# Reordering the opening of a pre-norm attention and GEGLU kernel: who makes the statistics, the masks and the first v tiles

## The chip, the cores and the metric

The kernel runs on one core of a Trainium2 chip. A core has five engines with a queue of instructions each: TensorE (PE in the profile, with PEld for its weight loads), VectorE (DVE), ScalarE (ACT), GpSimd (POOL) and SyncE (SP), which here only issues DMAs. Each engine works through its queue in order and waits on semaphores that others raise. The metric is the device time of one execution in microseconds. Before the change it is 279.58 us, the median of 3 runs (279.43 to 279.63).

## The reference

One layer over x of 2048 tokens by D = 640, in bf16, with 32 heads of Dh = 20 and a hidden width of 1536:

```python
qkv = layernorm(x) @ wqkv                     # split in q, k, v, per head
pq, pk = q_head @ w_phi[h], k_head @ w_phi[h] # a 20 x 20 matrix for each head
phi = concat(softmax(p), softmax(-p))         # for q and for k
kv  = sum over tokens of phi_k^T v            # per head, and z = sum of phi_k
o   = (phi_q kv) / (phi_q z + 1e-6)
h   = x + o @ wo
out = h + (gelu(ln(h) @ w_gate) * (ln(h) @ w_up)) @ w_down
```

## The kernel before

The tokens are cut into 16 tiles of 128. A tile is normalised with tokens on the partitions, transposed into `LN1T` (one buffer for four tiles), and then multiplied with weights. The 20 x 20 matrices of all heads are folded into the weights first: a block-diagonal matrix `BD` is made from w_phi and a mask (`bd`, L385), and `fold` (L214) multiplies the transposed weight (`WkT`, `WqT`) with it, 128 rows of the weight at a time (d = 0 to 4), six matmuls each. The result in PSUM (`wa`) is cast into `Wk2` or `Wq2` by ScalarE where d is in `KA` or `QA`, else by VectorE.

The order of work is written out by hand. Each engine gets its instructions in the order of the Python program, so the order of the calls sets what stands behind what on every queue. The part that the change touches is the opening (L394 to L430) and the loop over tiles (L435 to L482):

- Statistics. Tiles 0 and 1 (`ln_0`), and 2, 4, 5, 6, 7 (`ln_st`) get mean and variance from VectorE (`bn_stats`, L110, and the aggregate, L114). The reciprocal root is made by ScalarE for tiles 0 to 2 (L119, L120) and by GpSimd for the others (L122, L123). Tile 3 is different: `st3_act` (L369) lets ScalarE sum the squares and then the values of the tile (L372, the sums come out as `sm3`), and GpSimd makes mean and reciprocal root of them in five small steps (L374 to L378).
- Normalising and transposing. `ln_ap` (L257) lets VectorE (L139) or ScalarE (L134) write the normalised tile. `ln_tp` (L264) transposes it on TensorE (five matmuls against the identity, L147) into PSUM, from where ScalarE or, with a second argument of True, VectorE copies it into `LN1T` (L148). From tile 6 on the transposing is a DMA of the SP queue instead (L150).
- v. `v_part` (L284) issues the v matmuls of a tile for some of the five 128-row slices of the weight, `v_mm` (L279) all ten; `v_ev` (L293) lets ScalarE move the result to `vS`.
- Loads. SP issues the loads of x, W_v and w_phi in order (L171 to L181), then five DMA transposes of W_k (`load_T`, L186), then the rest of x (L417 to L419).
- PSUM. The tiles `tp`, `pv`, `pk`, `wa` take turns in four buffers (three from pass 4 on). A matmul into a buffer waits until the buffer's last contents have been read.
- The loop. Pass t runs k of tile t (`k_tile`, L302; ScalarE makes both exponentials, L307), a fold of W_q in the passes listed in `FQ`, accumulations of kv for earlier tiles in the passes of `KVG` (L340), v of tile t + 4, the normalising of tile t + 6 on ScalarE and its transpose on SP, the statistics of tiles t + 8 and t + 9 in even passes, and `k_norm` (L310), in which VectorE sums and inverts and VectorE and GpSimd multiply (L322). In passes 0 to 4 it also loads and transposes a slice of W_q (L464).

After the loop come the q products, attention and the feed-forward part (L615, L636), which the change does not touch.

Of the kernel before, what the change touches and what calls it, by code (L numbers as in the profile page):

```python
# [10 lines left out]
ALU = mybir.AluOpType  # L11
# [6 lines left out]
def kernel(  # L18
# [12 lines left out]
    nc = tc.nc  # L31
    P = 128
# [15 lines left out]
    VP = (0, 2, 4, 6, 9, 11)  # L48
    KA, QA = (1,3), (0,1,2,3,4)
    FQ = (4, 5, 6, 7, 8)  # L50

# [124 lines left out]
    nc.sync.dma_start(x_sb[0][:, 2:3, :], x_v[:, 2:3, :])  # L176
    nc.sync.dma_start(Wv[:, 2:4, :], w_v[:, 2:4, 2 * D:3 * D])
    nc.sync.dma_start(wphi, phi_v.rearrange("(c p) f -> p c f", p=P))
    nc.sync.dma_start(Wv[:, 4:5, :], w_v[:, 4:5, 2 * D:3 * D])
    nc.sync.dma_start(x_sb[0][:, 3:4, :], x_v[:, 3:4, :])  # L180
    nc.sync.dma_start(x_sb[1][:, 0:2, :], x_v[:, 4:6, :])  # L181
# [102 lines left out]
    def v_part(t, *cs):  # L284

        if 0 in cs:
            pv[t] = gtile("pv")
        for c in cs:
            for u in range(2):
                nc.tensor.matmul(pv[t][:, u, 0:HD], lhsT=lnT(t, c), rhs=Wv[:, c, u * HD:(u + 1) * HD],  # L290
                                 start=(c == 0), stop=(c == NC - 1))
# [77 lines left out]
    def st3_act(i):  # L369

        xt = x_sb[0][:, 3, :]
        nc.scalar.activation(sq3, xt, (ACTF.Square, ACTF.Identity)[i], accum_out=sm3[:, i:i + 1])  # L372
        if i == 1:
            nc.gpsimd.tensor_scalar(v3[:, 0:1], sm3[:, 1:2], sm3[:, 1:2], -1.0 / (D * D), op0=ALU.mult, op1=ALU.mult)  # L374
            nc.gpsimd.tensor_scalar_add(v3[:, 0:1], v3[:, 0:1], EPS)
            nc.gpsimd.tensor_scalar(v3[:, 1:2], sm3[:, 0:1], 1.0 / D, v3[:, 0:1], op0=ALU.mult, op1=ALU.add)
            nc.gpsimd.tensor_tensor(v3[:, 2:3], v3[:, 1:2], nhalf[:, 0:1], op=ALU.pow)
            nc.gpsimd.tensor_scalar(v3[:, 3:4], sm3[:, 1:2], 1.0 / D, None, op0=ALU.mult)  # L378
            lnp[3] = xt, v3[:, 3:4], v3[:, 2:3], None
# [4 lines left out]

    def bd(c0, c1):  # L385

        n = c1 - c0
        nc.vector.tensor_tensor(BD[:, c0:c1], wphi[:, c0:c1, None, :].to_broadcast([P, n, 8, Dh]),
                                hmask[:, c0:c1, :, None].to_broadcast([P, n, 8, Dh]), ALU.mult)

    def tr_c(t):
        transpose_to(LN1T[0][:, :, t * P:(t + 1) * P], xc[t], True, t == 1)
# [6 lines left out]
    v_part(0, 0, 1)  # L399
    tr_c(1)  # L400
    st3_act(0)
    v_part(0, 2, 3)
    bd(0, 3)
    ln_ap(2, on_pe=True)
    bd(3, NC)
    st3_act(1)
    v_part(1, 0, 1, 2, 3)
    ln_tp(2, True)
    v_part(0, 4)
    v_ev(0)  # L410
    ln_st(4, act=False)
    ln_ap(3, on_pe=True)
    v_part(1, 4)
    v_ev(1)
    v_part(2, *range(NC))
    v_ev(2)
    nc.sync.dma_start(x_sb[1][:, 2:4, :], x_v[:, 6:8, :])  # L417
    nc.sync.dma_start(x_sb[2], x_v[:, 8:12, :])
    nc.sync.dma_start(x_sb[3], x_v[:, 12:16, :])  # L419
    fold(WkT, Wk2, False, (0, 1, 2))  # L420
    ln_tp(3, False)
    fold(WkT, Wk2, False, (3, 4))
    v_mm(3)
    v_ev(3)
    ln_ap(4, on_pe=True)
    ln_tp(4)
    ln_st(5, act=False)
    ln_st(6)
    ln_ap(5, on_pe=True)
    ln_st(7)  # L430
# [4 lines left out]
    for t in range(NT):  # L435
# [14 lines left out]
        for i in KVG.get(t, ()):  # L450
            kv_tile(i)
        if t + 4 < NT:
            v_mm(t + 4)
            if t == 0:
                ln_tp(5)
        if t > 0 and t + 6 < NT:
            ln_ap(t + 6, on_act=True)
        if t + 4 < NT:
            v_ev(t + 4)
        if t % 2 == 0 and t + 8 < NT:  # L460
            ln_st(t + 8, t + 9)
        k_norm(t)
        if t < NC:
            load_T(WqT, 0, t)  # L464
        if t == 10:
# [299 lines left out]
```

## Time and profile before

| | |
|---|---|
| median of the runs | 279.58 us |
| span of the profiled execution, first to last instruction | 277.2 us |
| the median less the span | 2.4 us |
| PE, DVE, ACT, POOL busy, share of the span | 98%, 60%, 52%, 34% |
| granted TensorE clock in all slices | full |

For the profiled execution the profile gives the span as its own time; what lies around the span (launch and end) is known only as the difference to the median. A busy PE is not PE at its peak: a matmul's recorded duration holds the pipeline's latency, and two that follow each other overlap. So the starts of the groups are to be compared, not their durations. In a line of the timeline stand the start and the duration in us, the engine, the source line, the operation, output and input tiles with shapes, the count, and in brackets the idle time before it and what ended that. DMAs are told by the time from issue to landing.

### The profile page before, as it was taken

What the parts mean: (1) busy time and instruction counts of PE and PEld (TensorE: products, weight loads), DVE (VectorE), ACT (ScalarE), POOL (GpSimd) and SP (SyncE); (2) the same over time, 40 slices, a digit from 0 to 9 for tenths busy, and PEclk for the clock granted to TensorE, in tenths of its full rate; (3) what the DMA queues carried; (4) which work ended last, traced back from release to release, by engine and by line L of the source; (5) the groups of instructions that cost most, each with busy time, mean ns of one, the idle gap of its engine ahead of it and who ended that gap; (6) DMA issues with size and microseconds to landing.
All of it is one profiled execution on the core that took longest, in us unless ns stands there. A gap on an engine that the chain in (4) does not pass through costs nothing.

```text
span 277.2 us, 5817 instructions
## 1 busy us (share of the span) xinstructions
PE 271.6 (98%) x2337; PEld 172.1 (62%) x2337; DVE 167.3 (60%) x292; ACT 143.5 (52%) x239; POOL 94.7 (34%) x213
## 2 busy tenths in 40 slices
PE   7899999999999999999999999999999999999995
PEld 3677777764555887788754555675455567444574
DVE  6799999899496776675325757322666622233222
ACT  4879998778598755374524364413445440222200
POOL 4348997765202217365301353400226230000000
PEclk9999999999999999999999999999999999999999
DMA  7965732489730021324120213130022413000011
GB/s 204 192 232 112 99 74 47 44 256 393 255 102 0 4 47 36 85 49 77 30 65 2 47 27 63 32 88 33 14 36 25 73 25 95 26 0 0 0 50 47
DMA packets 42235, 21.37 MB, mean 77 GB/s; under 512 B 35040, under 2 KB 40416, under 8 KB 42208
## 3 DMA queue, kind: packets, MB, share of 16 engines
q1 hardware_dynamic: 42208, 21.01, 30.8%
q8 instruction: 18, 0.29, 0.5%
q14 instruction: 9, 0.07, 0.1%
HBM read 10.18 MB, written 2.62 MB: 46 GB/s over the span
## 4 chain that ended last, share of the span: by engine, by line
PE 87%; SPq 3%; DMA 3%; DVE 2%; ACT 2%; issue 1%
PE gu L615 38%; PE pd L636 19%; PE pq L362 8%; PE po L570 8%; PE pk L274 5%; PE pv L274 4%; PE ab L510 3%; PE kvp L340 2%; SPq L186 2%; DMA LN1T<-ln 2%; DVE stats L110 1%; DMA WkT<-in_A_wqkv_dram 1%; ACT E L307 1%; ACT ln L134 1%; PE wa L228 1%
## 5 line engine op out<-in xcount | busy, mean ns | idle before, releaser
L621 DVE TENSOR_TENSOR GT<-gu,g 128x512 bf16<-128x512 f32 (+1 forms) x60 | 34.4, 580 | 54.3 <-ACT g L618 54.1
L618 ACT ACTIVATE g<-gu 128x512 bf16<-128x512 f32 (+1 forms) x60 | 30.7, 512 | 69.3 <-PE gu L615 68.5
L615 PE MATMUL gu<-LN2T,Wg 128*128 128x512 bf16 (+1 forms) x300 | 61.9, 337 | 0.1
L615 PE MATMUL gu<-LN2T,Wu 128*128 128x512 bf16 (+1 forms) x300 | 61.8, 337 | 0.0
L636 PE MATMUL pd<-Wd,GT 128*128 128x320 bf16 (+2 forms) x396 | 53.8, 295 | 0.0
L636 PEld LDWEIGHTS <-GT 128*128 128x128 bf16 x396 | 37.9, 98 | 15.3 <-DVE GT L621 0.9
L615 PEld LDWEIGHTS <-Wu 128*128 128x128 bf16 x300 | 29.3, 98 | 22.6
L615 PEld LDWEIGHTS <-Wg 128*128 128x128 bf16 x300 | 28.3, 98 | 20.8
L274 PEld LDWEIGHTS <-LN1T 128*128 128x128 bf16 x290 | 27.9, 98 | 11.0 <-DMA LN1T<-ln 0.3
L322 POOL TENSOR_TENSOR vt<-vS,rs 128x672 bf16<-128x672 bf16 x22 | 29.1, 1344 | 9.1 <-DVE rs L318 7.4
L641 DVE TENSOR_TENSOR y<-pd,x_sb 128x640 bf16<-128x640 f32 (+3 forms) x18 | 13.5, 749 | 30.2 <-PE pd L636 30.2
L518 ACT COPY AB<-ab 128x704 f32<-128x704 f32 x28 | 19.6, 748 | 19.8 <-PE ab L510 19.6
L551 DVE TENSOR_TENSOR tt<-AB,w 128x1280 bf16<-128x1280 f32 x16 | 23.8, 1486 | 1.0 <-POOL w L544 0.9
L570 PE MATMUL po<-Wo,oT 128*128 128x320 bf16 x160 | 24.3, 299 | 0.0
L274 PE MATMUL pk<-Wk,LN1T 128*128 128x320 bf16 x160 | 24.0, 299 | 0.0
L314 DVE TENSOR_REDUCE sk<-E 128x64 f32<-128x1280 bf16 x16 | 22.9, 1434 | 1.2 <-ACT E L307 1.2
L362 PE MATMUL pq<-LN1T,Wq 128*128 128x512 bf16 x100 | 22.9, 379 | 0.0
L367 ACT ACTIVATE Eq<-pq 128x1024 bf16<-128x1024 f32 (+1 forms) x26 | 19.9, 830 | 2.4 <-PE pq L362 2.4
L307 ACT ACTIVATE E<-pk 128x640 bf16<-128x640 f32 x28 | 18.3, 716 | 4.5 <-PE pk L274 4.3
L570 PEld LDWEIGHTS <-oT 128*128 128x128 bf16 x160 | 15.6, 98 | 7.0 <-ACT oT L148 0.3
L274 PE MATMUL pv<-Wv,LN1T 128*128 128x320 bf16 x130 | 19.8, 299 | 0.2 <-DMA LN1T<-ln 0.2
L134 ACT ACTIVATE ln<-x_sb,v,rstd 128x640 bf16<-128x640 bf16 x14 | 12.9, 919 | 11.3 <-POOL v L598 11.1
(101 smaller groups left out, 268.1 us busy)
## 6 DMA issues: line engine op xcount, KB each, us to landing
out_dram<-y SPq DMA_DIRECT2D x15, 160.0 KB, 1.8
Wg<-in_B_w_gate_dram SPq DMA_DIRECT2D x1, 1920.0 KB, 9.4
Wu<-in_B_w_up_dram SPq DMA_DIRECT2D x1, 1920.0 KB, 15.3
Wd<-in_B_w_down_dram SPq DMA_DIRECT2D x1, 1920.0 KB, 7.9
x_sb<-in_A_x_dram SPq DMA_DIRECT2D x2, 640.0 KB, 5.5
Wo<-in_A_wo_dram SPq DMA_DIRECT2D x1, 800.0 KB, 11.1
x_sb<-in_A_x_dram SPq DMA_DIRECT2D x4, 160.0 KB, 3.1
Wv<-in_A_wqkv_dram SPq DMA_DIRECT2D x2, 320.0 KB, 4.1
```

The lines of the kernel that those rows point to most:

```text
L274: nc.tensor.matmul(ps[:, u, 0:HD], lhsT=lnT(t, c), rhs=W[:, c, u * HD:(u + 1) * HD], start=(c == 0), stop=(c == NC - 1))
L307: nc.scalar.activation(Ek[t][:, s, :].rearrange("p (u f) -> p u f", u=2), pk[:, :, 0:HD], ACTF.Exp, scale=((lnp[t][2], nrstd[t]) if t in C ...
L314: nc.vector.reduce_sum(sk, Ek[t].rearrange("p s (h f) -> p (s h) f", f=Dh), axis=AX.X)
L322: eng.tensor_tensor(vt[:, s], vS[t % 8], rs[:, s * H:(s + 1) * H, None].to_broadcast([P, H, VC]), ALU.mult)
L362: nc.tensor.matmul(pqs[j][:, i, :], lhsT=Wq2[:, kc, c * P:(c + 1) * P], rhs=LN1T[b][:, kc, :], start=(kc == 0), stop=(kc == NC - 1))
L367: nc.scalar.activation(Eq[j][:, :, s, :], pqs[j][:, 0:len(QG[j])], ACTF.Exp, scale=(1.0, -1.0)[s])
L551: nc.vector.tensor_tensor(tt.rearrange("p s (h f) -> p s h f", f=Dh), num, w[:, :, :, None].to_broadcast([P, 2, H, Dh]), ALU.mult)
L570: nc.tensor.matmul(po[:, u, 0:HD], lhsT=st[t][:, c, :], rhs=Wo[:, c, u * HD:(u + 1) * HD], start=(c == 0), stop=(c == NC - 1))
L615: nc.tensor.matmul(gu[:, i, 0:n], lhsT=W[:, c, f * P:(f + 1) * P], rhs=LN2T[b][:, c, a0:a1], start=(c == 0), stop=(c == NC - 1))
L618: nc.scalar.activation(g[:, 0:n], gu[:, 0, 0:n], ACTF.Gelu_apprx_tanh)
L621: nc.vector.tensor_tensor(st[b, "g", f][:, a0:a1], gu[:, 1, 0:n], g[:, 0:n], ALU.mult)
L636: nc.tensor.matmul(pd[:, u, n0:n1], lhsT=st[b, "g", f][:, tl * P:(tl + 1) * P], rhs=Wd[:, f, u * HD + n0:u * HD + n1], start=(f == 0), sto ...
```

## The change

- `st3_act`: ScalarE makes the sum of tile 3 first and the squares second. GpSimd's steps that need the sum alone (its square, the constant, the mean) are issued after the first; those that need the squares (the variance, the power) after the second.
- On SP, x of tile 3 is loaded ahead of w_phi and the last slice of W_v.
- `bd` takes an engine. Slices 0 to 2 of the block diagonals are made on GpSimd, ahead of the steps of tile 3; slices 3 and 4 stay on VectorE, now behind the normalising of tile 2.
- The transpose of tile 2 on TensorE comes after two instead of five slices of v of tile 1; the last slices of v of tiles 0 and 1 follow next to each other.
- Tiles 3 and 4 are normalised one after the other on VectorE. The transpose of tile 3 comes ahead of the folds of W_k, and its copy goes to VectorE. Tile 4 is transposed, and v of tile 3 made, between folds 2 and 3; v of tile 4 and the transpose of tile 5 come before the loop (they were in pass 0).
- The casts of W_k: ScalarE takes d = 0, 2, 4 instead of 1, 3.
- W_q is loaded in passes 0, 2, 4, 6, 8 and folded in 4, 6, 8, 10, 12, instead of 0 to 4 and 4 to 8.

```diff
-    KA, QA = (1,3), (0,1,2,3,4)
-    FQ = (4, 5, 6, 7, 8)
+    KA, QA = (0, 2, 4), (0, 1, 2, 3, 4)
+    FQ = (4, 6, 8, 10, 12)
...
+    nc.sync.dma_start(x_sb[0][:, 3:4, :], x_v[:, 3:4, :])
     nc.sync.dma_start(wphi, phi_v.rearrange("(c p) f -> p c f", p=P))
     nc.sync.dma_start(Wv[:, 4:5, :], w_v[:, 4:5, 2 * D:3 * D])
-    nc.sync.dma_start(x_sb[0][:, 3:4, :], x_v[:, 3:4, :])
...
-        nc.scalar.activation(sq3, xt, (ACTF.Square, ACTF.Identity)[i], accum_out=sm3[:, i:i + 1])
-        if i == 1:
-            nc.gpsimd.tensor_scalar(v3[:, 0:1], sm3[:, 1:2], sm3[:, 1:2], -1.0 / (D * D), op0=ALU.mult, op1=ALU.mult)
+        nc.scalar.activation(sq3, xt, (ACTF.Identity, ACTF.Square)[i], accum_out=sm3[:, i:i + 1])
+        if i == 0:
+            nc.gpsimd.tensor_scalar(v3[:, 0:1], sm3[:, 0:1], sm3[:, 0:1], -1.0 / (D * D), op0=ALU.mult, op1=ALU.mult)
             nc.gpsimd.tensor_scalar_add(v3[:, 0:1], v3[:, 0:1], EPS)
-            nc.gpsimd.tensor_scalar(v3[:, 1:2], sm3[:, 0:1], 1.0 / D, v3[:, 0:1], op0=ALU.mult, op1=ALU.add)
+            nc.gpsimd.tensor_scalar(v3[:, 3:4], sm3[:, 0:1], 1.0 / D, None, op0=ALU.mult)
+        else:
+            nc.gpsimd.tensor_scalar(v3[:, 1:2], sm3[:, 1:2], 1.0 / D, v3[:, 0:1], op0=ALU.mult, op1=ALU.add)
             nc.gpsimd.tensor_tensor(v3[:, 2:3], v3[:, 1:2], nhalf[:, 0:1], op=ALU.pow)
-            nc.gpsimd.tensor_scalar(v3[:, 3:4], sm3[:, 1:2], 1.0 / D, None, op0=ALU.mult)
...
-    def bd(c0, c1):
+    def bd(c0, c1, eng):
-        nc.vector.tensor_tensor(BD[:, c0:c1], wphi[:, c0:c1, None, :].to_broadcast([P, n, 8, Dh]),
+        eng.tensor_tensor(BD[:, c0:c1], wphi[:, c0:c1, None, :].to_broadcast([P, n, 8, Dh]),
...
+    bd(0, 3, nc.gpsimd)
     st3_act(0)
     v_part(0, 2, 3)
-    bd(0, 3)
     ln_ap(2, on_pe=True)
-    bd(3, NC)
+    bd(3, NC, nc.vector)
     st3_act(1)
-    v_part(1, 0, 1, 2, 3)
+    v_part(1, 0, 1)
     ln_tp(2, True)
+    v_part(1, 2, 3)
     v_part(0, 4)
     v_ev(0)
+    v_part(1, 4)
+    v_ev(1)
     ln_st(4, act=False)
     ln_ap(3, on_pe=True)
-    v_part(1, 4)
-    v_ev(1)
+    ln_ap(4, on_pe=True)
     v_part(2, *range(NC))
     v_ev(2)
...
+    ln_tp(3, True)
     fold(WkT, Wk2, False, (0, 1, 2))
-    ln_tp(3, False)
+    ln_tp(4, True)
+    v_mm(3)
+    ln_st(5, act=False)
+    v_ev(3)
     fold(WkT, Wk2, False, (3, 4))
-    v_mm(3)
-    v_ev(3)
-    ln_ap(4, on_pe=True)
-    ln_tp(4)
-    ln_st(5, act=False)
+    v_mm(4)
+    v_ev(4)
+    ln_ap(5, on_pe=True)
+    ln_tp(5)
     ln_st(6)
-    ln_ap(5, on_pe=True)
     ln_st(7)
...
-        if t + 4 < NT:
+        if 0 < t < NT - 4:
             v_mm(t + 4)
-            if t == 0:
-                ln_tp(5)
...
-        if t < NC:
-            load_T(WqT, 0, t)
+        if t % 2 == 0 and t < 2 * NC:
+            load_T(WqT, 0, t // 2)
```

More of the change, by code (lines that the diff above doesn't have):

```diff
@@ L451 @@
             kv_tile(i)
-        if t + 4 < NT:
+        if 0 < t < NT - 4:
             v_mm(t + 4)
-            if t == 0:
-                ln_tp(5)
         if t > 0 and t + 6 < NT:
             ln_ap(t + 6, on_act=True)
-        if t + 4 < NT:
+        if 0 < t < NT - 4:
             v_ev(t + 4)
```

## The prediction

> **What bounds the kernel now.** The page comes first: busy shares, then the chain that ended last.
>
> ```profile
> PE 271.6 (98%) x2337; PEld 172.1 (62%) x2337; DVE 167.3 (60%) x292; ACT 143.5 (52%) x239; POOL 94.7 (34%) x213
> ...
> PE 87%; SPq 3%; DMA 3%; DVE 2%; ACT 2%; issue 1%
> ```
>
> TensorE (PE) sets the time: 87% of the chain is its own work. Nearly all of the 13% elsewhere lies ahead of 33 us, where the change is made. So the question is how many idle PE spots it closes or opens. Next, the timeline of PE over the opening (start, duration, idle before):
>
> ```profile
> 7.15 1.79 PE L290 MATMUL pv<-Wv,LN1T 128*128 128x320 bf16 x12 [0.18 <-DMA Wv<-in_A_wqkv_dram]
> ...
> 11.17 1.11 PE L228 MATMUL wa<-BD,WkT 128*128 128x140 bf16 x18
> 12.40 0.45 PE L147 MATMUL tp<-ident,ln 128*128 128x128 bf16 x5
> 13.13 0.47 PE L228 MATMUL wa<-BD,WkT 128*128 128x140 bf16 x6 [0.28 <-DVE Wk L239]
> 13.77 0.49 PE L228 MATMUL wa<-BD,WkT 128*128 128x140 bf16 x6 [0.17 <-DMA WkT<-in_A_wqkv_dram]
> 14.10 1.52 PE L274 MATMUL pv<-Wv,LN1T 128*128 128x320 bf16 x10
> ...
> 20.18 1.52 PE L274 MATMUL pv<-Wv,LN1T 128*128 128x320 bf16 x10
> 21.54 1.52 PE L274 MATMUL pk<-Wk,LN1T 128*128 128x320 bf16 x10
> ...
> 31.77 0.95 PE L340 MATMUL kvp<-vt,E 128*64 128x84 bf16 x40
> 32.89 1.53 PE L274 MATMUL pv<-Wv,LN1T 128*128 128x320 bf16 x10 [0.16 <-DMA LN1T<-ln]
> ```
>
> Read differences of starts, since a duration holds pipeline latency: ten v or k matmuls cost 1.36 (20.18 to 21.54), six fold matmuls 0.32 (chain), a transpose group 0.28. Between 7.15 and 21.54 lie 76 v/k matmuls (10.3), four transpose groups (1.1) and five folds (1.6): 13.0 of 14.39. So PE idles 1.35 us there, nearly all between 10.9 and 14.1. From 21.54 to the q matmuls (60.79) lie 24 groups (32.6), five W_q folds (1.6) and 200 kvp matmuls (4.1): 38.3 of 39.25, 0.95 idle: 0.30 ahead of 32.89 (tile 9's transposed rows), 0.19 and 0.15 ahead of v10 and v11 at 39.16 and 42.34 (a PSUM buffer that ScalarE, ACT, had not emptied: vS ended 39.10), and 0.1 at each of three switches to kvp, which stay. The change can win at most 2 us.
>
> Third, the rows of tile 3's chain, which ends in the transpose at 12.40 (ACT, POOL and DVE, same columns).
>
> ```profile
> 8.27 0.74 ACT L372 ACTIVATE sq<-x_sb 128x640 bf16<-128x640 bf16 x1 [0.50 <-DMA x_sb<-in_A_x_dram]
> 10.06 0.27 POOL L374 TENSOR_SCALAR v<-sm 128x1 f32<-128x1 f32 x1 [3.43 <-ACT sq L372]
> 11.90 0.45 DVE L139 TENSOR_SCALAR ln<-x_sb,v 128x640 bf16<-128x640 bf16 x1 [1.12 <-POOL v L378]
> 7.49 0.66 DVE L388 TENSOR_TENSOR BD<-wphi,hmask 128x480 bf16<-128x480 bf16 x1
> ```
>
> x of tile 3 lands at 8.25, two ACT sums end at 9.97, five GpSimd (POOL) steps end at 11.87, VectorE (DVE) normalises till 12.35. The W_k casts on DVE queue behind that.
>
> **The change, part by part.** PE's work is the same to the matmul, so the sum is one of waits.
>
> *x of tile 3 moved past w_phi and Wv's last slice on SP.* Wv's second part lands at 7.1; next came w_phi 7.37, Wv 7.9, x3 8.25. In the new order I put x3 at 7.55 (0.37 to 0.5 for its 160 KB), w_phi 0.28 later, 7.85 (ends: 7.37 as before, 8.25 if it waits like x3 did), Wv 8.3; v needs that at 9.1, 0.8 spare. The W_k transposes and later x loads keep their places on SP (the next issue is at 5.20 in either order).
>
> *First three block diagonals on GpSimd.* No row shows this operation there. Nearest: GpSimd's vt, bf16 with one broadcast input, 1.31 for 672 elements, which for 480 is 0.94; its KV multiply, 0.89 for 420, gives 1.02. Ends: 0.66 (DVE's own row) and 2.7 (the rate of the short strided pr rows, 0.365 for 64). I take 1.0: 7.85 to 8.85. Behind it on GpSimd queue the sums of tile 3, then tile 4's rstd. It also meets DVE:
>
> ```profile
> 28.05 0.85 DVE L322 TENSOR_TENSOR vt<-vS,rs 128x672 bf16<-128x672 bf16 x1
> ...
> 54.93 1.31 POOL L322 TENSOR_TENSOR vt<-vS,rs 128x672 bf16<-128x672 bf16 x1
> 55.24 1.71 DVE L322 TENSOR_TENSOR vt<-vS,rs 128x672 bf16<-128x672 bf16 x1
> ```
>
> The same DVE multiply costs 0.85 against 1.71 when a GpSimd multiply runs; it ends 0.71 after GpSimd's, as if held till then. So bd(3,5), on DVE, waits for 8.85 and ends near 9.3 (PE's cover is the matmuls up to 9.66). Then the copy of tile 2's transpose ends 9.74: v of tile 2 starts 0.1 late.
>
> *Statistics of tile 3.* ACT's sum 7.79 (after tile 2's rstd) to 8.65, squares to 9.51. GpSimd, held about 0.15 by bd(3,5): 9.00, then 0.35 + 0.33 + 0.30 + 0.35 + 0.60 by starts of L374 to L378: 10.93 (was 11.87). DVE's ln 11.39. Only the second product waits for the squares (9.51 against 9.98), so the swap of sum and squares is covered; BD is now what is late: each 0.1 us more of it is 0.1 us on this path.
>
> *PE's new order.* Eight v matmuls 7.15 to 8.24; tile 2's transpose (ln 7.79 to 8.24) to 8.57; eight to 9.66; v2 9.74 to 11.10; transpose of tile 3 at 11.39, 0.29 idle; three folds 11.67 to 12.62 (W_k parts landed 9.7, 10.5, 11.8). Tile 4: pow 11.83, ln 12.28, then the DVE copy of tile 3, 12.65, which both frees PSUM and feeds v3: transpose 12.65, v3 12.93, two folds 14.29 (parts at 13.0, 13.7, so the 0.17 wait at 13.77 goes), v4 14.93, transpose 5 at 16.28 (DVE ln 16.25), k0 16.57, k1 17.93, v5 19.28, end 20.64 against 21.54. The same walk over the old order gives 21.42, 0.12 short of the trace; I take that off: **-0.78**. DVE loses one BD (0.66) and one cast (0.74) and gains two copies (0.41 each); ACT loses two copies (0.59), gains a cast (0.58). Both follow: ACT's ln of tile 7 starts 20.85 against 21.75. Were DVE not 0.6 lighter, ln 5, now just in time for transpose 5, would be late and stall PE.
>
> *W_q folds every second pass.* ACT costs per pass 1.30 (E) + 0.81 (ln) + 0.59 (vS) = 2.70, with a fold's cast 3.28; PE 2.72, with a fold 3.03. Five folds in a row put ACT behind by 0.25 each: the waits at 39.16 and 42.34. Alternated, one pass in two catches up: **-0.34** (0 to -0.34). The casts of passes 10 and 12 fall where ACT idles 0.59 to 0.91 a pass; without that cover they cost 0.58 each. On SP, five W_q transposes (1.28 issue each) leave gaps between tiles' transposes. Tile 9's took 4.89 to land, others 2.6: with 2.6 the 0.30 goes, with 4.89 it lands near 31.9 for a need at 31.3 and 0.6 stays; between them I take **-0.1**.
>
> Sum -1.2 us. The profiled execution's span is 277.21; the median 279.58 is 2.37 more, outside the span and untouched, so the difference is carried over: 278.4.
>
> *A rule against it.* The Trainium skill, page SBUF — State Buffer, section Who interferes with whom, says that DVE and GpSimd share a port pair, taken whole by whoever starts first, by `tensor_scalar` in a 2-port mode too. The trace's row first:
>
> ```profile
> 17.50 0.48 DVE L139 TENSOR_SCALAR ln<-x_sb,mv,rstd 128x640 bf16<-128x640 bf16 x1
> 17.60 0.21 POOL L122 TENSOR_SCALAR ve<-mv 128x1 f32<-128x1 f32 x1
> ```
>
> GpSimd ran its usual 0.21 inside a DVE ln, so nothing was held. By the rule, ln of tile 2 would hold BD to 8.23 and the sum would be about -0.85, 278.7; by the row, -1.2.
>
> **Rivals.**
> 1. *Little is left* (ln of tile 2 and BD do exclude each other, BD first). For it: GpSimd's ve beside the ln at 18.94 took 0.30, not 0.21. Against: the row above, and w_phi at 7.85 is after 7.79. Tile 2's transpose waits for 9.3, +0.65: **279.0**; with tile 9's 4.89 besides, 279.5.
> 2. *Slower: GpSimd is far slower on BD's short broadcast runs.* Place: BD, on the path to v2, transpose 3 and 4. It decides from 2.2 us (1.0 and the 1.2 won); at the 2.7 end it adds 1.7 to my sum: **280.1**. For it: pr's rate. Against: vt and KV, whose inner runs of 21 are BD's 20.
> 3. *All idle spots close* (BD 0.66, no late transpose): -1.7, **277.9**.
>
> **How the numbers follow.** My case, with its size errors (277.9 to 278.9): 0.53, all faster. Rival 1: 0.23, about the 0.2% line (0.56 us, what a measurement can tell from no change), 0.09 faster and 0.14 same. Rival 2, or one unseen wait of its size: 0.22, of it 0.04 same. Rival 3: 0.02. Faster 0.64, same 0.18, slower 0.18. The range reaches from rival 3 with 0.2 to spare, 277.7, to rival 2, 280.2; the likeliest case alone is 277.9 to 278.9.
>
> **What would show it.** BD on GpSimd near 7.85, 1.0 long; bd(3,5) on DVE ending after it; transpose 3 on PE near 11.4 and k of tile 2 at 20.6; no idle ahead of v10, v11. Wrong if BD takes over 2 us, or if w_phi lands after 8.5, or tile 2's transpose starts after 9.

## The result and the profile after

The changed kernel takes 278.67 us (median of 12 runs, 278.02 to 278.86); the kernel before, timed beside it, takes 279.44 (12 runs, 278.83 to 279.95). The ratio is 0.997, with a 95% interval of 0.996 to 0.9981: 0.77 us faster. A second measurement gave 0.9984 (0.9975 to 0.9993), 0.4 us. The forecast was 278.4, from 279.58.

The profiled execution has a span of 276.6 us and its own time is 278.31, so 1.7 us lie around the span. In all later runs it is 1.7 to 1.8. The prediction took 2.37 for it, the median less the span; the profiled execution of the kernel before was thus one of about 278.9, at the lower end of its spread. In spans the change gained 277.21 - 276.61 = 0.60 us.

The page of the changed kernel, busy shares and the chain that ended last:

```profile
PE 271.6 (98%) x2337; PEld 172.5 (62%) x2337; DVE 168.6 (61%) x292; ACT 142.6 (52%) x238; POOL 96.6 (35%) x214
...
PE 95%; DMA 1%; ACT 1%; DVE 1%; issue 0%; ACTq 0%; DVEq 0%
```

TensorE's own work is the same 271.6 us, and its share of the chain has gone from 87% to 95%. That sounds like 22 us and is 0.6: the old chain ran for long stretches through SP's queue and loads that were only just in time beside a busy TensorE. The share tells what ended last, not what can be won. For that the starts of TensorE's groups are needed (timeline of PE in the changed kernel: start, duration, idle before):

```profile
7.41 1.47 PE L290 MATMUL pv<-Wv,LN1T 128*128 128x320 bf16 x8
9.00 0.45 PE L147 MATMUL tp<-ident,ln 128*128 128x128 bf16 x5
9.29 2.61 PE L290 MATMUL pv<-Wv,LN1T 128*128 128x320 bf16 x18
11.74 0.44 PE L147 MATMUL tp<-ident,ln 128*128 128x128 bf16 x5
12.02 1.15 PE L228 MATMUL wa<-BD,WkT 128*128 128x140 bf16 x18
13.08 0.44 PE L147 MATMUL tp<-ident,ln 128*128 128x128 bf16 x5
...
15.35 1.52 PE L274 MATMUL pv<-Wv,LN1T 128*128 128x320 bf16 x10
16.71 0.44 PE L147 MATMUL tp<-ident,ln 128*128 128x128 bf16 x5
...
21.06 1.52 PE L274 MATMUL pk<-Wk,LN1T 128*128 128x320 bf16 x10
...
31.87 1.53 PE L274 MATMUL pv<-Wv,LN1T 128*128 128x320 bf16 x10
...
37.63 1.52 PE L274 MATMUL pv<-Wv,LN1T 128*128 128x320 bf16 x10
38.98 1.52 PE L274 MATMUL pk<-Wk,LN1T 128*128 128x320 bf16 x10
40.34 0.48 PE L228 MATMUL wa<-BD,WqT 128*128 128x140 bf16 x6
41.09 1.53 PE L274 MATMUL pv<-Wv,LN1T 128*128 128x320 bf16 x10 [0.27 <-DMA LN1T<-ln]
```

Eight v matmuls from 7.41 are worth 1.09, and the last four of them, of tile 1, wait 0.20 for VectorE's copy of tile 1 (they start at 8.16; the copy, shown below, ends at 8.10). So the transpose of tile 2 could have started near 8.72; it starts at 9.00 (forecast 8.29). From there the opening runs almost without a stop: the transpose of tile 3 at 11.74 waits for nothing, and only 0.11 is lost ahead of 13.08. k of tile 2 starts at 21.06, where the kernel before had 21.54 and the forecast 20.64. In the loop v of tiles 9, 10 and 11 (31.87 and 37.63 are the first and third) start with less than 0.1 of idle time ahead of them; but v of tile 12 at 41.09 starts 0.75 after the fold at 40.34, whose six matmuls are worth 0.32. The lost 0.43 is a new wait, for tile 12's transposed rows. The three stretches:

| us | before | after | gain | forecast |
|---|---|---|---|---|
| start to k of tile 2 | 21.54 | 21.06 | 0.48 | 0.78 |
| k of tile 2 to the first q matmul | 39.25 | 39.12 | 0.13 | 0.44 |
| from there to the end of the span | 216.42 | 216.43 | 0 | 0 |

Both parts gained, and both less than forecast. Why tile 2's transpose is late is seen on DVE and GpSimd of the changed kernel (timelines, same columns):

```profile
7.61 0.49 DVE L148 COPY LN1T<-tp 128x640 bf16<-128x640 bf16 x1 [0.43 <-PE tp L147]
8.02 0.92 DVE L139 TENSOR_SCALAR ln<-x_sb,mv,rstd 128x640 bf16<-128x640 bf16 x1
8.87 0.48 DVE L389 TENSOR_TENSOR BD<-wphi,hmask 128x320 bf16<-128x320 bf16 x1
...
11.03 0.45 DVE L139 TENSOR_SCALAR ln<-x_sb,v 128x640 bf16<-128x640 bf16 x1
...
7.78 0.99 POOL L389 TENSOR_TENSOR BD<-wphi,hmask 128x480 bf16<-128x480 bf16 x1 [0.53 <-DMA wphi<-in_A_w_phi_dram]
8.87 0.62 POOL L374 TENSOR_SCALAR v<-sm 128x1 f32<-128x1 f32 x1
...
10.42 0.57 POOL L379 TENSOR_TENSOR v<-v,nhalf 128x1 f32<-128x1 f32 x1
```

The normalising of tile 2 (second line, L139) takes 0.92 us where the same operation for tile 3 (at 11.03) takes 0.45. It ends at 8.94, 0.17 after GpSimd's block diagonals end at 8.77. The GpSimd side is as forecast: begun at 7.78 (7.85), 0.99 long (1.0), the power ended at 10.99 (10.93).

### The profile page after: what moved, and what is told of

Same layout as the page of the kernel before. It is cut to its first block, busy times and chain, and to the rows that moved or that the text cites. A ratio compares the mean times of both kernels' runs of the same rounds, so it can differ in the third digit from the quotient of the medians.

```text
span 276.6 us, 5825 instructions
## 1 busy us (share of the span) xinstructions
PE 271.6 (98%) x2337; PEld 172.5 (62%) x2337; DVE 168.6 (61%) x292; ACT 142.6 (52%) x238; POOL 96.6 (35%) x214
## 2 busy tenths in 40 slices
DMA packets 42235, 21.37 MB, mean 77 GB/s; under 512 B 35040, under 2 KB 40416, under 8 KB 42208
## 3 DMA queue, kind: packets, MB, share of 16 engines
HBM read 10.18 MB, written 2.62 MB: 46 GB/s over the span
## 4 chain that ended last, share of the span: by engine, by line
PE 95%; DMA 1%; ACT 1%; DVE 1%; issue 0%; ACTq 0%; DVEq 0%
PE gu L618 38%; PE pd L639 19%; PE pq L362 8%; PE po L573 8%; PE pk L274 7%; PE pv L274 6%; PE ab L513 3%; PE kvp L340 2%; PE wu L210 1%; DMA LN1T<-ln 1%; PE tp L147 1%; PE pv L290 1%; PE wa L228 1%; ACT E L307 0%; DVE ln L139 0%
## 5 line engine op out<-in xcount | busy, mean ns | idle before, releaser
L618 PEld LDWEIGHTS <-Wg 128*128 128x128 bf16 x300 | 28.4, 98 | 20.7
L307 ACT ACTIVATE E<-pk 128x640 bf16<-128x640 f32 x28 | 18.3, 710 | 4.4 <-PE pk L274 4.3
L134 ACT ACTIVATE ln<-x_sb,v,rstd 128x640 bf16<-128x640 bf16 x14 | 12.9, 919 | 11.4 <-POOL v L601 11.2
```

Source lines behind the costliest of these rows:

```text
L618: nc.tensor.matmul(gu[:, i, 0:n], lhsT=W[:, c, f * P:(f + 1) * P], rhs=LN2T[b][:, c, a0:a1], start=(c == 0), stop=(c == NC - 1))
```

## The experiments

The theory after the result: DVE's normalising and GpSimd's block-diagonal multiply exclude each other, and that costs about half of what the new opening could win; the spacing of W_q wins next to nothing since a new wait takes it back. The rivals: the opening was late for another reason (the first slow matmuls lasted longer in this profile, see `before_again`); or the spacing is the true gain, and the opening gave little. The kernels were timed in three groups, each beside runs of the kernel before on the same chip. "Tile 2" and "tile 3" are the starts of their transposes on TensorE, "loop" the time from k of tile 2 to the first q matmul, all in the profiled execution. The ratios are made from all runs and need not be those of the two medians.

| kernel | median us (runs) | ratio to before, 95% | tile 2 | tile 3 | k of tile 2 | loop |
|---|---|---|---|---|---|---|
| before, first profile | | | 8.77 | 12.40 | 21.54 | 39.25 |
| `before_again` | 278.89 (1) | | 8.99 | 12.47 | 21.50 | 39.23 |
| after, first profile | 278.67 (12) | 0.997 (0.996 to 0.9981) | 9.00 | 11.74 | 21.06 | 39.12 |
| `after_again` | 278.46 (11) | 0.9984 (0.9975 to 0.9993) | 8.72 | 11.84 | 21.37 | 38.96 |
| `bd_vector` | 278.04 (5) | 0.997 (0.9958 to 0.9982) | 8.87 | 11.81 | 21.08 | 39.06 |
| `bd_behind_ln3` | 278.21 (11) | 0.9971 (0.9959 to 0.9984) | 8.67 | 11.39 | 21.03 | 39.04 |
| `bd_vector_wq_before` | 278.12 (10) | 0.9965 (0.9952 to 0.9979) | 8.72 | 11.66 | 20.93 | 39.01 |
| `bd_twice` | 279.33 (12) | 1.0018 (1.001 to 1.0027) | 9.19 | 12.53 | 22.06 | 39.11 |
| `wq_as_before` | 278.44 (11) | 0.9984 (0.9974 to 0.9994) | 9.22 | 11.95 | 21.27 | 39.22 |
| `wq_only` | 278.58 (12) | 0.9999 (0.9989 to 1.0008) | 8.70 | 12.31 | 21.59 | 38.75 |
| `order_only` | 279.63 (12) | 1.0021 (1.0008 to 1.0033) | 9.09 | 13.27 | 22.57 | 39.03 |
| `stats_only` | 278.71 (12) | 0.9995 (0.9985 to 1.0005) | 9.62 | 12.98 | 21.89 | 39.02 |
| `wq_early` | 280.62 (6) | 1.0068 (1.0043 to 1.0092) | 9.10 | 11.83 | 21.15 | 42.83 |
| `both` | 280.16 (6) | 1.0048 (1.003 to 1.0066) | 8.72 | 11.44 | 21.16 | 40.97 |

The kernel before had a median of 278.85, 278.84 and 278.82 in the three groups.

### `after_again`: the changed kernel unaltered, beside the others

> The changed kernel once more, with a second profile. In its first profile the nine warm-up matmuls ran 0.42 us each to the end and v of tile 0 started at 6.58, where before's profile has 5.96; k of tile 2 started at 21.06 where 20.64 was forecast. Theory A (VectorE's ln of tile 2 is held while GpSimd makes BD): the ln takes about 0.9 again, the transpose of tile 2 starts 9.0 or later, k of tile 2 about 21.0, whatever the warm-up does. Theory B (the late start did it): with a warm-up that gets fast before 5 us, as in before's profile, the transpose of tile 2 starts near 8.3 and k of tile 2 near 20.6. Time: 0.997 of before in both, and this run shows how far two profiles of one kernel differ.

0.9984. Neither theory's profile came: v of tile 0 started late once more (6.58), and the normalising of tile 2 took 0.44, because this time it came first (DVE, then GpSimd):

```profile
8.03 0.44 DVE L139 TENSOR_SCALAR ln<-x_sb,mv,rstd 128x640 bf16<-128x640 bf16 x1
8.38 1.28 DVE L389 TENSOR_TENSOR BD<-wphi,hmask 128x320 bf16<-128x320 bf16 x1
...
8.24 1.07 POOL L389 TENSOR_TENSOR BD<-wphi,hmask 128x480 bf16<-128x480 bf16 x1 [0.99 <-DMA wphi<-in_A_w_phi_dram]
```

w_phi landed 0.46 later than in the first profile, behind the start of the normalising, which then took its plain 0.44. The transpose of tile 2 is earlier for it (8.72), but GpSimd's whole chain to tile 3 starts later, tile 3's transpose follows at 11.84 after 0.35 of idle time, and k of tile 2 at 21.37, 0.31 later than in the first profile. Whichever of the two comes first, the opening pays: tile 2 waits or tile 3 does. The line on the 320-element DVE multiply (1.28 for 0.48) is a hold as well, and ends 0.35 after GpSimd's.

### `bd_vector`: the block diagonals on DVE, behind tile 4's aggregate

```diff
-    bd(0, 3, nc.gpsimd)
     st3_act(0)
...
     ln_st(4, act=False)
+    bd(0, 3, nc.vector)
     ln_ap(3, on_pe=True)
```

> The changed kernel, but block diagonals 0 to 2 on VectorE, behind tile 4's aggregate, not on GpSimd. Theory A: with GpSimd idle VectorE's ln of tile 2 takes 0.44, the transpose of tile 2 starts by 8.5, GpSimd's steps of tile 3 end near 10.5 and the transpose of tile 3 starts near 11.2 instead of 11.74; k of tile 2 near 20.5, the time 0.4 to 0.6 us under the changed kernel. Theory B (late start): no gain but what the warm-up decides; the transpose of tile 3 stays near 11.7 and the time is that of the changed kernel or, as VectorE has 0.58 more to do, 0.1 to 0.3 us above it.

0.997; of its five times three lie below the lowest of the 22 of `after_again` and `wq_as_before` in the same group (278.14). DVE's rows:

```profile
8.17 0.44 DVE L139 TENSOR_SCALAR ln<-x_sb,mv,rstd 128x640 bf16<-128x640 bf16 x1
8.53 0.48 DVE L389 TENSOR_TENSOR BD<-wphi,hmask 128x320 bf16<-128x320 bf16 x1
...
9.75 0.88 DVE L110 BATCH_NORM_STATS2 stats<-x_sb 128x6 f32<-128x320 bf16 x2
10.67 0.21 DVE L114 BATCH_NORM_AGGREGATE mv<-stats 128x2 f32<-128x12 f32 x1
10.79 0.60 DVE L389 TENSOR_TENSOR BD<-wphi,hmask 128x480 bf16<-128x480 bf16 x1
11.31 0.44 DVE L139 TENSOR_SCALAR ln<-x_sb,v 128x640 bf16<-128x640 bf16 x1
```

With no GpSimd multiply in the way, both operations take their plain time (0.44, 0.48), but the multiply of 480 elements does not fall into a hole: DVE has tile 4's statistics to make until 10.88. Tile 3's are ready at 10.69, and the multiply holds its normalising back till 11.31. TensorE loses 0.21 us of that by the starts (v of tile 2 is through at 11.60, the transpose of tile 3 starts at 11.81). The time is what theory A said; its profile (8.5, 11.2 and 20.5 for tile 2, tile 3 and k of tile 2) did not come, since v started late here too. All stands 0.15 later than in `bd_vector_wq_before` from tile 2's transpose on, and k of tile 2 at 21.08 is no earlier than in the changed kernel's first profile. So here the gain shows in the times, of which there are five, and not in the profile.

### `bd_behind_ln3`: the same, one place later

```diff
     ln_ap(3, on_pe=True)
+    bd(0, 3, nc.vector)
     ln_ap(4, on_pe=True)
```

(and the call on GpSimd taken out, as above)

> The changed kernel with block diagonals 0 to 2 on VectorE between the normalising of tiles 3 and 4. Theory A: tile 3's ln is no longer behind them, so its transpose starts when v of tile 2 ends, 11.6 with the late warm-up, 0.2 earlier than with the block diagonals behind tile 4's aggregate, and the time is 0.1 to 0.3 us under that version. Rival: held GpSimd power of tile 4 and the wait of the first fold for the block diagonals (ready near 11.9) cost it back: the same time, 0.997 of before.

0.9971, no different from `bd_vector`. The transpose of tile 3 comes at 11.39 without a wait. That is the forecast's number by chance: there tile 3's normalising set it, here the end of v of tile 2. And the first fold now waits 0.18 for the block diagonals, and the transpose of tile 4 0.25, as GpSimd's step L123 took 0.86 instead of 0.56 beside DVE's multiply. So on DVE the place is worth nothing more: what tile 3 wins, the folds and tile 4 give back.

### `bd_twice`: the GpSimd multiply made twice

```diff
     bd(0, 3, nc.gpsimd)
+    bd(0, 3, nc.gpsimd)
     st3_act(0)
```

> The changed kernel with the GpSimd block diagonals 0 to 2 made twice in a row, a cost of 0.99 to 1.07 more on GpSimd. Theory A (the block diagonals stand on the path to tile 3's transpose one for one): GpSimd's power for tile 3 ends 1.0 later, the transpose of tile 3 starts near 12.8, k of tile 2 near 22.2, the time 0.9 to 1.0 us above the changed kernel and 0.3 to 0.5 above before. Theory B (there is slack behind them, tile 2's v being the bound): 0.5 us or less. For the shared port: if VectorE's ln of tile 2 is held by one GpSimd instruction only, it takes up to 0.95 as in the changed kernel; if the second goes ahead of it too, up to 2.0 and the transpose of tile 2 starts near 10.

1.0018, against 0.9984 for the unaltered kernel in another group: 0.0034 of 279 is 0.95 us for 1.07 us more of GpSimd (2.06 in all). GpSimd, then DVE:

```profile
7.96 2.06 POOL L389 TENSOR_TENSOR BD<-wphi,hmask 128x480 bf16<-128x480 bf16 x2 [0.71 <-DMA wphi<-in_A_w_phi_dram]
...
8.15 0.98 DVE L139 TENSOR_SCALAR ln<-x_sb,mv,rstd 128x640 bf16<-128x640 bf16 x1
9.05 1.31 DVE L389 TENSOR_TENSOR BD<-wphi,hmask 128x320 bf16<-128x320 bf16 x1
```

The normalising was held by the first of the two GpSimd multiplies only (0.98, ended 9.13; the first multiply ended 8.95), the 320-element multiply by the second (1.31). The transposes of tiles 2, 3 and 4 stand at 9.19, 12.53, 14.09. Against the first profile of the changed kernel tile 3's is 0.79 later (some slack is used up first), tile 4's 1.01 and k of tile 2 1.00; against `after_again`, where w_phi had landed late, each is 0.7 later. So the delay is on tile 3's path and nearly all of it is passed on. That GpSimd's multiply lies on the path of the opening is thus shown, and with it how far rival 2 would have gone: at 2.06 us the kernel is 0.5 us slower than before. By the same slope, an estimate, it would be no faster than before from about 1.5 us on, where rival 2 had put 2.2.

### `wq_as_before`: the new opening with the old passes of W_q

```diff
-    FQ = (4, 6, 8, 10, 12)
+    FQ = (4, 5, 6, 7, 8)
...
-        if t % 2 == 0 and t < 2 * NC:
-            load_T(WqT, 0, t // 2)
+        if t < NC:
+            load_T(WqT, 0, t)
```

> The changed opening with W_q loaded in passes 0 to 4 and folded in 4 to 8 as before. Theory A (spacing the folds is worth 0.34, the PSUM waits ahead of v10 and v11): the waits of about 0.15 to 0.2 ahead of v10 and v11 return and the time is 0.3 us above the changed kernel, 0.998 of before. Rival (spacing is worth nothing: the wait moved to tile 12's transposed rows, 0.43 in the changed kernel's profile): within 0.15 us of the changed kernel, with idle time ahead of v9 to v11 in place of v12.

0.9984, the same as `after_again` beside it (278.44 and 278.46). The waits ahead of v of tiles 9, 11 and 12 are back (0.26, 0.20, 0.15), the last in place of the 0.43 for tile 12's late rows. (The prediction and the expectations call the groups at 39.16 and 42.34 v10 and v11. They are v of tiles 11 and 12: pass t makes v of tile t + 4, and they stand in passes 7 and 8.) The normalising of tile 2 was held once more:

```profile
8.02 1.14 DVE L139 TENSOR_SCALAR ln<-x_sb,mv,rstd 128x640 bf16<-128x640 bf16 x1
```

### `wq_only`: the spacing of W_q alone

In the kernel before:

```diff
-    FQ = (4, 5, 6, 7, 8)
+    FQ = (4, 6, 8, 10, 12)
...
-        if t < NC:
-            load_T(WqT, 0, t)
+        if t % 2 == 0 and t < 2 * NC:
+            load_T(WqT, 0, t // 2)
```

> The kernel before with only the W_q loads and folds spaced. Theory A: no idle time ahead of v10 and v11, 0.3 us under before (0.999). Rival: a tile's transposed rows come late somewhere from v9 to v13 and the time is before's within 0.15 us. The opening up to k of tile 2 is before's, 21.5, in both.

0.9999, though the medians differ by 0.27. Its profiled execution has the shortest loop of all (38.75, waits of 0.07 ahead of tiles 9 and 12) and a time of 278.57; but its twelve times fall in two groups, seven from 278.28 to 278.59 and five from 278.97 to 279.5. What separates them no profile here shows. The profiles on the whole agree with the timings that little is to be had: the six with spaced folds have loops of 38.75 to 39.12, mean 39.01; the six with the old passes, `before_again` among them, 39.01 to 39.25, mean 39.13.

### `bd_vector_wq_before`: `bd_vector` with the old passes of W_q

```diff
-    FQ = (4, 6, 8, 10, 12)
+    FQ = (4, 5, 6, 7, 8)
...
-    bd(0, 3, nc.gpsimd)
     st3_act(0)
...
     ln_st(4, act=False)
+    bd(0, 3, nc.vector)
```

(and the loads of W_q as in `wq_as_before`)

> The block diagonals on VectorE behind tile 4's aggregate, and W_q loaded and folded as before. Theory A (spacing W_q is worth nothing measurable, the change's gain is all in the opening): 0.997 of before, as with spaced W_q, with idle time of 0.2 ahead of v10 and v11. Rival (spacing is worth 0.3 us): 0.998 of before.

0.9965, the lowest ratio of all, though its interval overlaps those of `bd_vector` and `bd_behind_ln3`: with the block diagonals on DVE, too, the spacing is worth nothing that these runs can tell, so what gain can be told comes from the opening. k of tile 2 starts at 20.93. Beside `wq_as_before` this run also gives the plainest view of what the place of the multiply is worth, as the two kernels differ in nothing else and start v of tile 0 at the same 6.58: tile 2's transpose 8.72 against 9.22, tile 3's 11.66 against 11.95, k of tile 2 20.93 against 21.27, 0.34 us.

### `order_only`: the new order on TensorE without the new statistics

The order of the calls, the places of the copies and the casts of the change; but x of tile 3 loaded last, squares first, block diagonals on DVE ahead of tile 2's normalising, and W_q as before. Against the changed kernel, beside those undone hunks:

```diff
-    bd(0, 3, nc.gpsimd)
     st3_act(0)
     v_part(0, 2, 3)
+    bd(0, 3, nc.vector)
     ln_ap(2, on_pe=True)
```

> The kernel before with only the order of the opening changed (v of tiles 3 and 4 and their transposes ahead of the last W_k folds, the casts and copies moved, tiles 3 and 4 normalised back to back); statistics of tile 3, loads, block diagonals on VectorE and W_q stay as before. Theory A (the order alone makes the gain, since the idle spots were waits inside the folds): no idle time ahead of folds 3 and 4, the transpose of tile 3 near 12.3 as before because its statistics come no earlier, k of tile 2 near 21.2 to 21.5, the time 0.2 to 0.4 us under before. Theory B (order needs the earlier statistics): the PE now waits for tile 3's transpose ahead of all folds, about 1.0 from 11.3 to 12.3, and the time is before's or up to 0.5 us above it.

1.0021, slower than before. Tile 3 on PE, on ACT and on DVE:

```profile
13.27 0.45 PE L147 MATMUL tp<-ident,ln 128*128 128x128 bf16 x5 [1.28 <-DVE ln L139]
...
9.14 0.74 ACT L372 ACTIVATE sq<-x_sb 128x640 bf16<-128x640 bf16 x1 [1.22 <-DMA x_sb<-in_A_x_dram]
...
12.76 0.45 DVE L139 TENSOR_SCALAR ln<-x_sb,v 128x640 bf16<-128x640 bf16 x1 [1.65 <-POOL v L378]
```

With tile 3's transpose ahead of the folds, TensorE has nothing to do till it comes, and stands still for 1.28 us by the profile (1.45 by the starts). The three folds had been its cover. But 0.87 us of this is a late load: x of tile 3, issued at 4.25 as in the kernel before, landed at 9.12 here and at 8.25 there, and ScalarE's squares start behind it. The rest, 0.58, is the order's. How the 0.6 us in the times divide is not known; the twelve lie between 278.75 and 280.19.

### `stats_only`: the new statistics in the old order

The load of x of tile 3 ahead of w_phi, the sum ahead of the squares, and the five GpSimd steps in their new order, in the kernel before:

```diff
+    nc.sync.dma_start(x_sb[0][:, 3:4, :], x_v[:, 3:4, :])
     nc.sync.dma_start(wphi, phi_v.rearrange("(c p) f -> p c f", p=P))
...
-    nc.sync.dma_start(x_sb[0][:, 3:4, :], x_v[:, 3:4, :])
...
-        nc.scalar.activation(sq3, xt, (ACTF.Square, ACTF.Identity)[i], accum_out=sm3[:, i:i + 1])
+        nc.scalar.activation(sq3, xt, (ACTF.Identity, ACTF.Square)[i], accum_out=sm3[:, i:i + 1])
...
```

> The kernel before with only the load of tile 3's x moved ahead and its sum made before its squares. Theory A: GpSimd's steps end near 11.0 instead of 11.87, but in the old order the folds 0 to 2 stand ahead of tile 3's transpose till 12.2 and the waits of folds 3 and 4 (W_k's parts, the cast of fold 0) stay: the transpose of tile 3 starts 0.1 to 0.2 earlier and the time is within 0.2 us of before. Theory B (the statistics are what the opening waited for): 0.5 us or more under before.

0.9995, within the noise. GpSimd's last step ends at 10.94 (11.87 before), but w_phi comes later for DVE (DVE, then PE):

```profile
8.54 0.66 DVE L389 TENSOR_TENSOR BD<-wphi,hmask 128x480 bf16<-128x480 bf16 x1 [1.00 <-DMA wphi<-in_A_w_phi_dram]
...
9.62 0.45 PE L147 MATMUL tp<-ident,ln 128*128 128x128 bf16 x5 [0.76 <-DVE ln L139]
```

DVE's first multiply waits 1.00 us for w_phi with tile 2's normalising queued behind it, and tile 2's transpose goes to 9.62. The size of that wait belongs to this execution: w_phi landed at 8.45, in the nine profiles of other kernels with the same order of loads at 7.70 to 8.16. What tile 3 gains, tile 2 loses, and tile 3's transpose, behind the folds in this order, comes at 12.98. So neither half gains anything on its own in these runs: the new order needs the earlier statistics, and the earlier x3 needs the block diagonals out of tile 2's way.

### `wq_early` and `both`: W_q's slices transposed ahead of the loop

These tried to take tile 12's late rows away by having the W_q transposes out of the loop; `both` has the block diagonals as in `bd_behind_ln3` besides.

```diff
     nc.sync.dma_start(x_sb[3], x_v[:, 12:16, :])
+    load_T(WqT, 0, *range(NC - 1))
...
-        if t % 2 == 0 and t < 2 * NC:
-            load_T(WqT, 0, t // 2)
+        if t == 4:
+            load_T(WqT, 0, NC - 1)
```

> The changed kernel with four of the five W_q transposing loads issued on SP right behind the last x load (13 to 19 us, where SP is idle) and the fifth in pass 4. Theory A (a tile's transposed rows come late because W_q transposes share the queue): tiles 7 to 13 land 2.6 after their issue, the idle time ahead of v12 (0.27 to 0.43) goes, the time 0.3 us under the changed kernel. Rival (the delay comes with something else that uses the DMA engines at 28.6 and 39.3, whichever transposes are in flight): some tile's rows still take 3.4 to 4.2, and the time is the changed kernel's within 0.15 us. Tile 6's rows might be held up behind the fourth W_q part by up to 0.5, against 0.7 to spare.

> The version the runs point to: block diagonals 0 to 2 on VectorE behind tile 3's normalising, so that neither VectorE's ln of tile 2 nor GpSimd's steps of tile 3 are held by them, and the W_q loads early. Theory A: transpose of tile 3 by 11.6 with the late warm-up, 11.2 with the early one, k of tile 2 at 20.9 or 20.5, no idle time ahead of v12; 0.6 to 0.8 us under the changed kernel, 0.9955 of before. Rival: block diagonals on VectorE at 11.2 to 11.8 hold GpSimd's power for tile 4 and delay its transpose by 0.3, and the transposed rows stay late: the time of the run with the block diagonals on VectorE behind tile 4's aggregate, 0.997 of before.

Both are slower, 1.0068 and 1.0048. In `wq_early` SP, then PE:

```profile
13.40 8.57 SPq L186 DMA_TRANSPOSE WqT<-in_A_wqkv_dram  x4
22.09 4.01 SPq L150 DMA_TRANSPOSE LN1T<-ln  x3
...
24.86 1.90 PE L274 MATMUL pv<-Wv,LN1T 128*128 128x320 bf16 x10 [2.19 <-DMA LN1T<-ln]
26.55 2.87 PE L274 MATMUL pk<-Wk,LN1T 128*128 128x320 bf16 x10
29.22 1.56 PE L274 MATMUL pv<-Wv,LN1T 128*128 128x320 bf16 x10
```

Four transposes kept SP's queue for 8.57 us (issued one by one in the loop they take 1.27 each), landing 7 to 8 us after their issue for the first three; the loads of x issued just ahead were moving at the time, at up to 457 GB/s by the trace in 18 to 21 us. Tile 6's rows, queued behind, were issued at 22.09 instead of 19.12, and TensorE stood still for 2.19 us (2.35 by the starts). `both` had the same wait (2.02, by the starts 2.19) and a clean opening, k of tile 2 at 21.16. The theory behind both runs fell as well: with no W_q transpose near them (the last landed 2.4 us before tile 12's rows were issued), tile 12's rows still took 3.19 us in both, tile 13's 4.22 and 4.15. The rest of `wq_early` is told in the last section. Whether W_q could be had early at another place was not tried.

### `before_again`: the kernel before, profiled once more

> The kernel before once more, for a second profile. If the moment at which the warm-up matmuls get fast is chance, this profile can show them slow to 6 us as the changed kernel's profiles do, with v of tile 0 at 6.58 and k of tile 2 at 21.8 to 22.1 instead of 21.54; if it belongs to the kernel, v of tile 0 starts at 5.96 to 6.02 again.

A second profile of the kernel before was to tell whether the late start of v in the changed kernel's profiles belongs to the change. The first nine matmuls (a warm-up on zeros) and the next rows of PE, first profile of before, then this one:

```profile
1.24 3.55 PE L210 MATMUL wu<-zero 128*128 128x512 bf16 x9 [1.24 <-DVE zero L195]
...
5.96 0.72 PE L290 MATMUL pv<-Wv,LN1T 128*128 128x320 bf16 x4 [0.35 <-ACT LN1T L148]
```

```profile
1.24 4.00 PE L210 MATMUL wu<-zero 128*128 128x512 bf16 x9 [1.24 <-DVE zero L195]
...
6.31 0.72 PE L290 MATMUL pv<-Wv,LN1T 128*128 128x320 bf16 x4 [0.35 <-ACT LN1T L148]
```

The same kernel starts v of tile 0 0.35 later, with no consequence: k of tile 2 at 21.50, span 277.16 instead of 277.21. In the kernel before, the lateness ends in the wait for tile 3. So the moment differs between executions of one kernel. But 6.31 is neither of the two numbers expected, and whether the change has a part in it stays open: in the four profiles with the old order on TensorE v of tile 0 starts at 5.96 to 6.31, in the ten with the new order at 6.45 to 6.58, though TensorE's instructions up to there are the same. No profile shows the new order with an early start.

What it does in the changed kernel can be told. Tile 2's transpose missed its forecast by 0.71 us (9.00 for 8.29). With v of tile 0 at the same 6.58 and the normalising not held, it starts at 8.72 in `after_again`, `bd_vector_wq_before` and `both`. So some 0.43 us is the late start, by way of the copy of tile 1 (7.61, the first line of DVE's rows of the changed kernel), and the hold adds 0.28. An earlier start alone would not have helped: a held normalising ends 0.17 to 0.18 after GpSimd's multiply in all four profiles that have one, begun 0.02 to 0.24 behind it.

## Why the prediction was right, and where it was wrong

**The size of the gain.** 278.4 was forecast and 278.67 measured, with a gain of 1.2 forecast and 0.77 and 0.4 measured. The direction and the opening's path were right, the size was not: against the profiled execution, the forecast -1.2 stands beside -0.60. That the two times lie only 0.27 apart is in part luck. The median of three that the sum started from, 279.58, is 0.14 to 0.76 above every later median of the same kernel, and a start too high made up for a gain too large. From the profiled execution's own time, 278.9, the sum gives 277.7, the lower end of the range.

**"GpSimd ran its usual 0.21 inside a DVE ln, so nothing was held" failed.** The row was right and the inference from it was wrong. A 128x1 step of 0.21 us is no test of a 480-element multiply with two inputs in memory. In the three profiles of the changed opening where the multiply came first (the first of after, `wq_as_before`, `wq_early`: 0.92, 1.14, 1.15) and in `bd_twice` (0.98) the normalising was held until the multiply had ended; where the normalising came first, or no GpSimd multiply was there, it took 0.44 or 0.45. Even the small step was a chance pick: beside tile 3's normalising at 11.03 the same kind of step (L122) took 0.40. The Trainium skill had it right: SBUF — State Buffer, section Who interferes with whom, has the two engines exclude each other when a `tensor_scalar` uses both ports, and has the order of issue decide who waits. Its sum, -0.85 and 278.7, supposed that the normalising would be first. Which is first hangs on when w_phi lands, and the profiles with a GpSimd multiply have it at 7.70 to 8.16 with the normalising ready near 8.0: in one of the five it was first. That its 278.7 is the measured time is luck, too. What the hold and GpSimd's 0.99 us cost together, beside the multiply on DVE: `bd_vector` against `after_again`, 278.04 against 278.46 in the same group, is 0.4 us (five runs against eleven); `bd_vector_wq_before` against `wq_as_before` is 0.34 at k of tile 2. Over all profiles the two kinds overlap: k of tile 2 stands at 20.93 to 21.16 with the multiply on DVE and at 21.06 to 21.37 with it once on GpSimd. What the hold costs without the rest no run here isolates.

**Rival 1 was this mechanism, and its price was too high.** Its 279.0 lies 0.33 above the measured time, the forecast 0.27 below. It put the transpose of tile 2 at 9.3 and +0.65 on the end. It came at 9.00, 0.71 after the forecast's 8.29, but at the transpose of tile 3 only 0.35 were left (11.74 against 11.39): the 0.29 that the walk had idle there took most of the rest. Another 0.08 was lost ahead of the transpose of tile 4. The walk was 0.12 short of the trace by its own account, and 0.35 + 0.08 - 0.12 = 0.31 stands against the 0.30 between -0.78 and -0.48.

**The opening's mechanism was right.** The statistics of tile 3 took the forecast way: 0.99 for GpSimd's multiply (1.0), its step L374 held by DVE's 320-element multiply (0.62 instead of 0.27; 0.15 of hold was forecast), the power ended at 10.99 (10.93), tile 3 normalised by 11.48 (11.39). The sentence that "each 0.1 us more of it is 0.1 us on this path" was nearly borne out by `bd_twice`, 0.95 us for 1.07 in the times and 0.7 to 1.0 in the profiles. `order_only` and `stats_only` show why the parts are not to be priced one by one: 0.6 us slower (0.0021 of 279, some of it perhaps the late load) and no change, each alone. What the walk lacked was the late start: it took v over from the kernel before, and the first matmuls were slow for longer in every profile of the new order.

**"Alternated, one pass in two catches up: -0.34", and "I take -0.1" for tile 9, failed in sum.** 0.44 was forecast for the loop and 0.13 came. The reading of the waits was right: with the new passes v of tile 11 starts without one, v of tile 12 has 0.07 ahead of it in `wq_only`, and tile 9's rows landed after 3.83 us in the changed kernel (forecast between 2.6 and 4.89) and in time. What was late next was not named: in the changed kernel tile 12's rows, issued at 37.52, landed after 3.52 instead of 2.6, for 0.43 us of idle time at the very group whose 0.15 had been counted as won. It took 3.37 to 3.52 again in `after_again`, `bd_vector`, `bd_twice` and `bd_behind_ln3` (0.27 to 0.42). In times the spacing was worth nothing in three pairs (one of them across two groups). Why these rows are slow is not settled. It isn't the W_q transpose issued 1.25 us behind them: `wq_only` has that too and there they landed after 2.62, and `wq_early` and `both` have it not and there they landed after 3.19. What goes with it in all fourteen profiles: in the seven with late rows a fetch of instructions on queue 14 starts 1.74 to 1.80 us after the rows are issued (39.26 in the changed kernel); in the seven where they land after 2.57 to 2.62 it starts ahead of them, by 0.9 in `wq_only` (37.16) and by 1.2 in the six with the old passes. No kernel moved that fetch alone, so this is not shown to be the cause.

**Rivals 2 and 3 did not come.** GpSimd's multiply has the rate of the `vt` and KV rows, not that of the short strided ones. And part of the idle time that rival 3 closed is still there.

**A version that came out ahead of both.** With the block diagonals on DVE, the new opening takes 278.04, 278.21 and 278.12 us in three forms, against 278.85, 278.82 and 278.82 for the kernel before beside them. Only the first was timed beside the changed kernel, which took 278.46 there; in its first measurement the changed kernel had the ratio to before that `bd_vector` has, 0.997.

## What to carry to other kernels

Before work is moved to an idle engine, it is to be asked which operation of a busy engine will run beside it, and that pair has to be found in the trace at a like size; a tiny operation that ran freely proves nothing. An idle engine need not be the cheaper place: the multiply took 0.60 to 0.65 us on DVE, where it delayed tile 3's normalising by 0.5 or the folds and tile 4 by 0.2 each, and yet the kernel was no slower than with 0.99 us and a hold from idle GpSimd, and in the one pair timed side by side 0.4 us faster. A wait that is taken away at one place is won only if the next operand is early enough too, so the arrival times of the next three or four have to be read before a gain is put down for the first.

## What the runs showed of the hardware

- **A hold lasts one instruction.** With two GpSimd multiplies in a row, DVE's normalising got in after the first, and the second held the next DVE instruction (`bd_twice`: 0.98 and 1.31 for 0.44 and 0.48). DVE's two-input multiply in turn holds small GpSimd steps: L374 took 0.62 instead of 0.27, L123 0.86 instead of 0.56.
- **A gap of 2.35 us without a matmul was followed, in one profile, by half the clock.** In `wq_early` matmuls of 320 columns start 0.136 us apart up to 25.82, then 0.267 apart until 29.22, that is for 3.40 us, then 0.136 again. The trace by stretches (columns: PE, PEld, DVE, ACT and POOL busy, granted clock, DMA share, GB/s):

```profile
24.80:25.50 0.70, 0.64 (x5) 0.49 (x6) 0.70 (x3) 0.07 (x1) 0.70 (x1) 1.00 1.07 211
25.50:26.20 0.70, 0.70 (x6) 0.46 (x5) 0.70 (x3) 0.00 (x0) 0.70 (x2) 0.77 0.16 33
26.20:27.00 0.80, 0.80 (x5) 0.45 (x3) 0.80 (x4) 0.20 (x1) 0.74 (x1) 0.50 0.93 184
...
29.80:30.50 0.70, 0.70 (x8) 0.50 (x6) 0.00 (x0) 0.70 (x2) 0.70 (x1) 1.00 0.00 0
```

  The clock fell a microsecond after the work had come back, and cost 13 intervals of 0.13, 1.7 us: this execution took 282.11, with a mean granted clock of 0.994. The six times of the kernel lie at 280.27 to 280.68 (four) and at 282.11 and 282.45, the last with 0.994 too. In the profiled execution of `both`, 2.19 us without a matmul left the clock full, but another of its six, of 281.47, has 0.994 as well. No other run on record has less than 0.998. So the drop goes with such a gap in some executions, one by its trace and two more by their granted clock, and not in others. The Trainium skill, TensorE: Matmul & The Clock Gate, section HAM oscillation — how this bites in real kernels, warns of gaps above about 3.4 us; here the drop followed a shorter one.
- **Long DMA packets beside instruction fetches.** In the profiles of the kernel before, 256-byte packets of the transposes took up to 1.70 and 1.74 us from 29.7 on, 0.55 us after a fetch on queue 8 began (29.14, 29.13); in the changed kernel 1.37 from 29.2, after a fetch at 28.64; in `wq_early` up to 2.41 from 18.3 to 20.7, but there the first of them began 0.45 ahead of the fetch at 18.74, so that fetch cannot have started it. That was read off the packets; no run took the fetch away, and a cause is not shown.
- **The first matmuls are slow for a time that differs between profiles.** The 512-column matmuls at the start are 0.427 us apart and go over to 0.216 after seven intervals in the first profile of before and after eight or more in `before_again` and the changed kernel, though the profile gives a granted clock of 1.00 throughout. The new opening passes on such a difference (`bd_vector` stands 0.15 behind `bd_vector_wq_before` from the first v matmuls to k of tile 2); the kernel before absorbed it.
